# Fused attention and gated hidden layer on one core: weights prepared two per operation in the order of their use, and four of the second chunk's heads on split parts

## The chip, the cores and the metric

One core of a Trainium2 chip runs one program. The metric is the device time of an execution in microseconds. TensorE (PE) multiplies, VectorE (DVE), ScalarE (ACT) and GpSimd (POOL) work on tiles of 128 partitions, SyncE (SP) issues most transfers.

## What is computed

```python
def _attn_ref(q, k, v, n_sink, window):       # q, k, v: (4, 8, 768, 64)
    scores = scale * np.matmul(q, k.transpose(0, 1, 3, 2))
    keep = is_sink | in_window                # n_sink 4, window 128
    scores = np.where(keep, scores, -1000000000.0)
    ...
    return np.matmul(a, v).astype(np.float32) # a: softmax of scores
def _moe_ref(x, w_a, w_b, w_out):             # 3072 tokens, 512 -> 1536 -> 512
    a = x @ w_a
    b = x @ w_b
    return (a * b @ w_out).astype(np.float32)
```

The attention's output, with heads side by side, is the x of the hidden layer. Weights arrive as 64-bit floats (pairs of 32-bit words).

## The kernel before

The 24 tiles of 128 queries are cut into eight chunks: (batch, first tile, tiles) = (0, 0, 4), (0, 4, 2), then six of three tiles. Chunk 0's attention runs alone. After that the hidden layer of a chunk (`moe`) runs with the attention of the next one threaded through it: `between` takes steps of the attention's generator between the products of the hidden units j = 0 to 11.

Precision comes in two ways. The exact way (`parts_exact`) multiplies in 32-bit float. The split way (`parts_split`) rounds an operand to a shorter format (F32R), keeps the rest as a second operand of that format, and adds two products. The hidden layer always uses split operands: three products for each 128 x 128 block of weights (high x high, high x low, low x high). Attention of chunks 0 and 1 is exact, of the others split. In the split way GpSimd makes the high and low parts of k, q and v (`prep_kq`, `prep_v`, tiles ks, qh, ql, vv, vs), and after the transposes of the probabilities ACT makes their high part (tile pt) and DVE their low part.

A weight is a tile of 128 x 512 for each of a, b and o and each hidden unit: 36 in all. `weight_bits` makes a 32-bit float's words out of the 64-bit one's (a shift L297 and a mask L299 on DVE, a conversion L298 on ACT), `weight_sum` adds (L307, DVE), `weight_high` rounds (L313, ACT), and `weight_low` subtracts (L318, DVE). `weights_to` issues one weight's stages at a time, each stage a step behind the one before it, in the order a 0, b 0, o 0, a 1, b 1, o 1 and so on. It is called in the last part of chunk 0's attention (every third step from step 18) and in chunk 0's hidden layer (three times for each hidden unit, through `weights_ahead`). The product of a and b of unit j is used by o's products one unit later, so that o j is wanted after b j+1. All engines work through their queues in order; the order is written by the program and a scheduler that moves independent work ahead.

The PSUM tile t is one bank: in the exact way its first half takes transposes, and its second half (chunk 1) value and sink products. In chunk 1 the value products (L601) and sink products (L623) therefore also appear under the name t.

Of the kernel before, what the change touches and what calls it, by code (L numbers as in the profile page):

```python
# [33 lines left out]
STEP0, STEPS = 18, 3  # L34
AHEAD, LOADS = 3, 9
D0, D1, D2 = 1, 2, 3
WARM = 8
H_MIN = 1.375 * 2.0 ** -12
# [172 lines left out]
UNITS = ((0, 4, "BA"), (1, 2, "AB"), (3, 5, "AB"))  # L211
GROUPS = ((0, 0, 2, 0), (1, 2, 2, 1), (2, 5, 0, 2), (-1, 4, 1, 0))
# [5 lines left out]
class Fast:  # L218
# [14 lines left out]
    def consts(self):  # L233
        nc, cp = self.nc, self.cp
        self.m0 = cp.tile([P, P], F32, name="m0")
        self.m1 = cp.tile([P, SW], F32, name="m1")
        self.mg = cp.tile([P, SW], F32, name="mg")
        self.rel = rel = self.at.tile([P, SW], F32, tag="p", name="rel")
        self.col = col = self.at.tile([P, SW], F32, tag="p", name="col")
        it = dict(allow_small_or_imprecise_dtypes=True)  # L240
        s, b = slice(P, P + NS), slice(P + NS, SW)
        nc.gpsimd.iota(rel[:, b], pattern=[[-1, P]], base=0, channel_multiplier=1, **it)
        nc.gpsimd.iota(rel[:, :P], pattern=[[-1, P]], base=P, channel_multiplier=1, **it)
        nc.gpsimd.iota(rel[:, s], pattern=[[1, NS]], base=0, channel_multiplier=0, **it)
# [7 lines left out]
        self.wt, self.raw, self.wf, self.unchecked = {}, {}, {}, []  # L252
# [34 lines left out]
    def load_weight(self, kind, j):  # L287
        raw = self.wp.tile([P, 2 * DM], I32, tag=f"w_{kind}{j}", name=f"raw_{kind}{j}")
        self.nc.sync.dma_start(raw, self.src(kind)[j].bitcast(I32))
        self.raw[kind, j] = raw  # L290

    def weight_bits(self, kind, j):
        nc, pin = self.nc, self.tc.keep_in_program_order
        rv = self.raw[kind, j].rearrange("p (n c) -> p n c", c=2)
        lo, hi = rv[:, :, 0], rv[:, :, 1]
        f = self.io([P, DM], I32, f"wf_{kind}{j}")
# [4 lines left out]
        self.wf[kind, j] = f  # L301

    def weight_sum(self, kind, j):

        f = self.wf[kind, j]
        lo = self.raw.pop((kind, j)).rearrange("p (n c) -> p n c", c=2)[:, :, 0]
        self.tc.keep_in_program_order(self.nc.vector.tensor_tensor(f, f, lo, op=ALU.add))  # L307
        self.wf[kind, j] = f.bitcast(F32)

    def weight_high(self, kind, j):  # L310
        w = self.wp.tile([P, 2, DM], F32R, tag=f"w_{kind}{j}", name=f"w_{kind}{j}")
        self.wt[kind, j] = (w[:, 0, :], w[:, 1, :])
        self.tc.keep_in_program_order(self.nc.scalar.copy(w[:, 0, :], self.wf[kind, j]))  # L313

    def weight_low(self, kind, j):
        wh, wl = self.wt[kind, j]
        self.tc.keep_in_program_order(
            self.nc.vector.tensor_tensor(wl, self.wf.pop((kind, j)), wh.bitcast(F32), op=ALU.subtract))  # L318
# [71 lines left out]
    def attention(self, b, t0, nt, xf, exact=False, alone=False):  # L390
        parts = self.parts_exact(b, t0, nt, xf, alone) if exact else self.parts_split(b, t0, nt, xf)
        late = [i for i in range(nt) if t0 + i >= 2]
        units = [(h, i) for h in range(H) for i in range(nt)]
        return self.pipeline(units, nt, late, *parts, 3 if alone else 2, 2 if exact else 4, 2 if alone else 1)

    def parts_split(self, b, t0, nt, xf):
# [4 lines left out]
        units = [(h, i) for h in range(H) for i in range(nt)]  # L401
        tps, preps, state, sc, vss, avs, skt = [], {}, {}, {}, {}, {}, {}

        def do_prep(h):
            if h < H:
# [30 lines left out]
        def transposes(h, i):  # L436
            p = state.pop((h, i))
            t = t0 + i
            u = f"{tag}_{h}_{i}"
            n = units.index((h, i))  # L440
            if not tps:
                tps.append(self.ps.tile([P, 4, P], F32, tag="t", name=f"t{u}"))
            tp = tps[0][:, 2 * (n % 2):2 * (n % 2) + 2, :]
            c1, c2, order = UNITS[i]
            parts = {"A": p[:, :P], "B": p[:, P + NS:]}
            if t == 0:
                parts["B"] = p[:, :P]
                order = "B"
            for k, o in enumerate(order):
                nc.tensor.transpose(tp[:, k, :], parts[o], self.ident)  # L450
            n = len(order)
            hs, ls = (self.pt_split()[:, part, c1:c1 + (n - 1) * (c2 - c1) + 1:c2 - c1, :] for part in range(2))
            nc.scalar.copy(hs, tp[:, :n, :])  # L453
            nc.vector.tensor_tensor(ls, tp[:, :n, :], hs.bitcast(F32), op=ALU.subtract)  # L454

        def av(h):
            vv = preps[h][3]
            ps = self.ps.tile([P, 4 * P], F32, tag="av", name=f"av{tag}_{h}")
            pt = self.pt_split()
            products = []  # L460
            for k, sl, ns, c in GROUPS:
# [11 lines left out]
            nc.vector.tensor_tensor(x[mn, 2 * P:], ps[mn, 3 * P:], x[mn, 2 * P:], op=ALU.add)  # L473
# [14 lines left out]
        def sinks_av(g, pr):  # L488
            n = len(late) * P
            ps = self.ps.tile([P, 3 * P], F32, tag="av", name=f"sk{tag}_{g}_{pr}")  # L490
# [6 lines left out]
    def parts_exact(self, b, t0, nt, xf, alone):  # L497
# [7 lines left out]
        units = [(h, i) for h in range(H) for i in range(nt)]  # L505
        preps, state, sc, vss, pts, skt, bank = {}, {}, {}, {}, {}, {}, {}

        def half_bank(second, name):

            if not bank:  # L510
                bank[0] = self.ps.tile([P, 4, P], F32, tag="t", name=name)
            return bank[0][:, 2:] if second else bank[0][:, :2]

        def do_prep(h):
            if h >= H:
                return
# [53 lines left out]
        def transposes(h, i):  # L570
# [16 lines left out]
        def av(h):  # L587
# [3 lines left out]
            else:  # L591
                ps = half_bank(1, f"av{tag}_{h}")
# [12 lines left out]
        def sinks_t(pr):  # L605
# [3 lines left out]
            else:  # L609
                tp = half_bank(0, f"skt{tag}_{pr}")  # L610
# [6 lines left out]
        def sinks_av(pr, _):  # L617
# [3 lines left out]
            else:  # L621
                ps = half_bank(1, f"sk{tag}_{pr}")
# [6 lines left out]
    def pipeline(self, units, nt, late, do_prep, scores, transposes, av, sinks_t, sinks_av, lag, group, early):  # L629

        for h in range(early):
# [39 lines left out]
    def moe(self, row, nt, xf, between, weights_ahead, last, weights_split):  # L671
# [6 lines left out]
        def half(kind, j):  # L678
            wh, wl = self.wt[kind, j]
# [9 lines left out]
        def project(j, gh, gl):  # L689
            wh, wl = self.wt["o", j]  # L690
# [41 lines left out]
    def run(self, scalars, verdict):  # L732
        chunks = CHUNKS
        order = [(k, j) for j in range(NJ) for k in "abo"]
        done, loaded = [0], [0]

        def weights_to(n, ahead):
            while loaded[0] < min(n + ahead, len(order)):
                self.load_weight(*order[loaded[0]])
                loaded[0] += 1  # L740
            while done[0] < min(n + D2, len(order) + D2):
# [8 lines left out]
        pairs = [self.wp.tile([P, 2, nt * P], F32, tag=f"w_{k}{NJ - 1}", name=f"xf0_{k}") for k in "bo"]  # L750
        xf = [x[:, i, :] for x in pairs for i in range(2)]
# [5 lines left out]
        for k, _ in enumerate(first, 1):  # L757
            if k >= STEP0 and (k - STEP0) % STEPS == 0:
                weights_to(done[0] + 1 - D2, 4 + D2)
        for c, (b, t0, nt) in enumerate(chunks):  # L760
            gen = None
            if c + 1 < len(chunks):
                nb, nt0, nnt = chunks[c + 1]
                nxf = self.new_xf(c + 1)
                gen = self.attention(nb, nt0, nnt, nxf, exact=c == 0)
                steps = H * nnt + (6 if c else 5)
            taken = [0]

            def between(s):
                if gen is None:  # L770
                    return
                want = min(steps, -(-steps * (s + 1) // (3 * NJ - 3)))
# [94 lines left out]
```

## Time and profile before

| | |
|---|---|
| median of 3 runs | 802.18 us (800.78 to 804.23) |
| the profiled execution | 800.92 us, span 799.0 us |
| TensorE | busy 785.5 us (98%), granted clock 0.999 |
| VectorE | busy 433.3 us (54%) |
| ScalarE | busy 475.8 us (60%) |
| GpSimd | busy 307.1 us (38%) |

Busy times are from start to end of each instruction; neighbours on one engine overlap a little. Chunk 0's attention fills the first 47 us or so, chunk 0's hidden layer reaches to 179 us, and the other seven chunks take the rest. The whole-program shares of VectorE and ScalarE average a dense first 160 us with a looser remainder.

### The profile page before, as it was taken

To read this page: it belongs to the slowest core of one execution; us is meant where nothing else is said; L and a number is where in the kernel's file an instruction comes from. 1 tells how busy PE (TensorE), PEld (TensorE's weight loads), DVE (VectorE), ACT (ScalarE), POOL (GpSimd) and SP (SyncE) were. 2 spreads that over 40 slices of the span, in tenths; PEclk is the share of its full clock that TensorE was granted. 3 is DMA by queue.
4 is the path that set the end of the run, shared out by engine and by line. 5 is a ranking of instruction groups with operands and counts; after the bars stand their busy time and mean duration, and the time that the engine had idled before them with its cause. 6 is when DMAs were issued, how large, how long until landed. Compare 5 with 4: busy or idle time off the path is not lost.

```text
span 799.0 us, 13573 instructions
## 1 busy us (share of the span) xinstructions
PE 785.5 (98%) x4457; PEld 697.2 (87%) x4457; DVE 433.3 (54%) x1485; ACT 475.8 (60%) x1384; POOL 307.1 (38%) x425
## 2 busy tenths in 40 slices
PE   8989999999999999999999999999999999999997
PEld 5657777779899999999999999999999999999996
DVE  6889988835654565445653555535654457430101
ACT  5877676527764676467764777646764677641111
POOL 1111100416672644546642565606635366201120
PEclk9999999999999999999999999999999999999999
DMA  8868610122221242313333143322333132000001
GB/s 314 298 228 319 205 30 1 41 82 77 61 73 38 79 128 90 104 55 117 102 102 116 42 123 109 91 77 64 114 119 102 54 107 61 1 14 28 1 1 42
DMA packets 44779, 76.12 MB, mean 95 GB/s; under 512 B 4640, under 2 KB 24224, under 8 KB 44704
## 3 DMA queue, kind: packets, MB, share of 16 engines
q1 hardware_dynamic: 41648, 69.70, 27.2%
q10 hardware_dynamic: 3024, 5.51, 1.8%
q8 instruction: 36, 0.59, 0.3%
q14 instruction: 39, 0.32, 0.1%
q0 software_dynamic: 32, 0.00, 0.0%
HBM read 68.90 MB, written 6.29 MB: 94 GB/s over the span
## 4 chain that ended last, share of the span: by engine, by line
PE 92%; DVE 4%; ACT 3%; DMA 1%; issue 1%; POOL 0%; DVEq 0%; POOLq 0%; ACTq 0%
PE a L685 25%; PE o L694 24%; PE b L685 24%; PE t L450 4%; PE s L418 4%; PE av L466 3%; PE s L547 2%; PE av L601 2%; PE t L584 1%; PE t L601 1%; PE sk L491 1%; ACT p L425 1%; DVE g L710 0%; ACT xf L471 0%; DVE xf L472 0%
## 5 line engine op out<-in xcount | busy, mean ns | idle before, releaser
L685 PE MATMUL a<-xh,w_a 128*128 128x384 f32 (+2 forms) x768 | 218.2, 345 | 1.3 <-ACT xh L666 1.0
L685 PE MATMUL b<-xh,w_b 128*128 128x384 f32 (+2 forms) x768 | 215.8, 343 | 0.0
L694 PE MATMUL o<-w_o,gh 128*128 128x512 f32 x576 | 186.9, 404 | 0.0
L685 PEld LDWEIGHTS a<-xh,w_a 128*128 128x128 f32 x768 | 138.8, 188 | 8.2 <-issue 1.7
L715 POOL TENSOR_TENSOR gl<-g,gh 128x384 fp32r<-128x384 f32 (+1 forms) x70 | 68.2, 974 | 201.1 <-ACT gh L713 198.3
L685 PEld LDWEIGHTS b<-xh,w_b 128*128 128x128 f32 x768 | 138.8, 188 | 4.7 <-issue 1.2
L710 DVE TENSOR_TENSOR g<-b,g 128x384 f32<-128x384 f32 (+2 forms) x96 | 53.4, 557 | 146.2 <-PE b L685 133.3
L685 PE MATMUL b<-xl,w_b 128*128 128x384 f32 (+2 forms) x384 | 129.2, 336 | 0.0
L685 PE MATMUL a<-xl,w_a 128*128 128x384 f32 (+2 forms) x384 | 129.2, 336 | 0.0
L694 PEld LDWEIGHTS o<-w_o,gh 128*128 128x128 f32 x576 | 104.0, 188 | 19.3 <-issue 0.8
L694 PE MATMUL o<-w_o,gl 128*128 128x512 f32 x288 | 113.6, 395 | 0.0
L713 ACT CAST gh<-g 128x384 fp32r<-128x384 f32 (+2 forms) x96 | 49.3, 514 | 78.4 <-DVE g L710 76.5
L704 ACT COPY g<-a 128x384 f32<-128x384 f32 (+2 forms) x96 | 45.2, 471 | 72.9 <-PE a L685 70.3
L429 ACT ACTIVATE p<-p,st 128x128 f32<-128x128 f32 (+1 forms) x144 | 71.4, 496 | 26.4 <-DVE st L428 25.5
L425 ACT ACTIVATE p<-p,st 128x128 f32<-128x128 f32 (+1 forms) x144 | 71.6, 497 | 8.5 <-DVE st L423 8.4
L685 PEld LDWEIGHTS a<-xl,w_a 128*128 128x128 f32 x384 | 72.4, 189 | 2.3
L685 PEld LDWEIGHTS b<-xl,w_b 128*128 128x128 f32 x384 | 72.4, 188 | 1.6
L453 ACT CAST pt<-t 128x128 fp32r<-128x128 f32 (+1 forms) x144 | 50.4, 350 | 39.1 <-PE t L450 37.3
L454 DVE TENSOR_TENSOR pt<-t,pt 128x128 fp32r<-128x128 f32 (+1 forms) x144 | 57.2, 397 | 20.7 <-ACT pt L453 19.2
L694 PEld LDWEIGHTS o<-w_o,gl 128*128 128x128 f32 x288 | 54.1, 188 | 13.1 <-DVE gl L715 0.8
L568 POOL COPY sc<-p 128x8 f32<-128x8 f32 x32 | 15.7, 490 | 128.7 <-ACT p L563 86.6
L423 DVE CUSTOM_DVE_ANT_0 p<-s,mg 128x264 f32<-128x264 f32 x96 | 41.1, 429 | 34.2 <-PE s L418 34.0
(141 smaller groups left out, 1287.3 us busy)
## 6 DMA issues: line engine op xcount, KB each, us to landing
qr<-in_qT_dram SPq DMA_DIRECT2D x48, 192.0 KB, 2.6
raw_a<-in_wa_dram SPq DMA_DIRECT2D x12, 512.0 KB, 6.5
raw_b<-in_wb_dram SPq DMA_DIRECT2D x12, 512.0 KB, 6.6
raw_o<-in_wo_dram SPq DMA_DIRECT2D x12, 512.0 KB, 6.6
chk_a<-in_wa_dram SPq DMA_DIRECT2D x24, 256.0 KB, 2.7
chk_b<-in_wb_dram SPq DMA_DIRECT2D x24, 256.0 KB, 2.7
chk_o<-in_wo_dram SPq DMA_DIRECT2D x24, 256.0 KB, 2.8
out_dram<-os ACTq DMA_DIRECT2D x21, 256.0 KB, 2.1
```

Source lines behind the costliest of these rows:

```text
L418: nc.tensor.matmul(ps[:, :w], lhsT=q[:, i * P:(i + 1) * P], rhs=ks[:, c0:c0 + w], start=m == 0, stop=m == 1)
L423: nc.vector.tensor_tensor_reduce(out=p[:, :w], in0=ps[:, :w], in1=m, scale=-0.125, scalar=BIG, op0=ALU.add, op1=ALU.min, accum_out=st[:, 0:1])
L425: nc.scalar.activation(p[:, :w], p[:, :w], AF.Exp, bias=st[:, 0:1], scale=-1.0, accum_out=st[:, 1:2])
L429: nc.scalar.mul(p[:, :w], p[:, :w], st[:, 3:4])
L453: nc.scalar.copy(hs, tp[:, :n, :])
L454: nc.vector.tensor_tensor(ls, tp[:, :n, :], hs.bitcast(F32), op=ALU.subtract)
L685: nc.tensor.matmul(ps[:, :n], lhsT=w[:, ksl], rhs=x[:, :n], start=kk == 0 and i == 0, stop=kk == NK - 1 and i == 2)
L694: nc.tensor.matmul(outs[i], lhsT=g[:, sl], rhs=w, start=j == 0 and k == 0, stop=j == NJ - 1 and k == 2)
L704: nc.scalar.copy(g[:, :n], pa[:, :n])
L710: nc.vector.tensor_tensor(g[:, :n], pb[:, :n], g[:, :n], op=ALU.mult)
L713: nc.scalar.copy(gh[:, :n], g[:, :n])
L715: e.tensor_tensor(gl[:, :n], g[:, :n], gh[:, :n].bitcast(F32), op=ALU.subtract)
```

## The change

Weights are sorted by their use (a 0, b 0, a 1, b 1, o 0, a 2, b 2, o 1, ...). Numbers 2 to 27 of that order are prepared two per operation, 1024 elements instead of 512, through one shared temporary tile; the first two and the last eight stay single. A pair shares one tile. Preparation begins at step 24 of chunk 0's attention instead of 18. In chunk 1, heads 0 to 3 stay exact and heads 4 to 7 take the split way, with one bank for transposes (first half) and products (second half); the four exact heads are spread over the first 18 of the hidden layer's calls and the split ones over the rest.

```diff
-STEP0, STEPS = 18, 3
-AHEAD, LOADS = 3, 9
-D0, D1, D2 = 1, 2, 3
+STEP0, STEPS = 24, 3
+AHEAD, LOADS = 1, 11
+DELAY = 3
+SINGLE, PAIRS = 2, 14
+EXACT, MID = 4, 18
...
+UNITS = {3: ((0, 4, "BA"), (1, 2, "AB"), (3, 5, "AB")), 2: ((0, 4, "BA"), (1, 5, "AB"))}
+GROUPS = {
+    3: ((0, 0, 2, 0), (1, 2, 2, 1), (2, 5, 0, 2), (-1, 4, 1, 0)),
+    2: ((0, 0, 2, 0), (1, 5, 1, 1), (-1, 4, 1, 0)),
+}
...
+        if n == 2:
+            if self.temp is None:
+
+                self.temp = self.wp.tile([P, 2 * DM], I32, tag=f"w{3 * NJ // 2 - 2}", name="wf")
+            f = self.temp
...
+    def attention_of_two(self, b, t0, nt, xf):
+
+        bank = {}
+        first = self.attention(b, t0, nt, xf, exact=True, heads=range(EXACT), bank=bank)
+        second = self.attention(b, t0, nt, xf, heads=range(EXACT, H), bank=bank)
+        next(first)
+        yield
+        n = EXACT * nt
+        for k in range(n + (H - EXACT) * nt + 6):
+            next(first, None)
+            if k >= n - 2 and k != n - 1:
+                next(second, None)
+            yield
...
-        order = [(k, j) for j in range(NJ) for k in "abo"]
+
+        order = self.order = sorted(((k, j) for j in range(NJ) for k in "abo"), key=lambda w: 3 * w[1] + (0, 1, 5)["abo".index(w[0])])
...
-                for d, stage in ((D2, self.weight_low), (D1, self.weight_high), (D0, self.weight_sum), (0, self.weight_bits)):
-                    if 0 <= k - d < len(order):
-                        stage(*order[k - d])
                 done[0] += 1
+                singles = lambda d: 0 <= k - d < len(order) and k - d not in wide
+                if singles(3):
+                    self.weight_low(k - 3, 1)
+                if k % 2 == 0 and k - 2 in wide:
+                    self.weight_low(k - 2, 2)
+                if singles(2):
+                    self.weight_high(k - 2, 1)
+                if singles(1):
+                    self.weight_sum(k - 1, 1)
+                if k % 2 == 1 and k - 1 in wide:
+                    self.weight_sum(k - 1, 2)
+                    self.weight_high(k - 1, 2)
+                if singles(0):
+                    self.weight_bits(k, 1)
+                if k % 2 == 0 and k in wide:
+                    self.weight_bits(k, 2)
...
-                weights_to(done[0] + 1 - D2, 4 + D2)
+                weights_to(done[0] + 1 - DELAY, 4 + DELAY)
...
-                gen = self.attention(nb, nt0, nnt, nxf, exact=c == 0)
-                steps = H * nnt + (6 if c else 5)
+                gen = (self.attention if c else self.attention_of_two)(nb, nt0, nnt, nxf)
+                steps = H * nnt + 6
...
-                weights_to(max(s + AHEAD, done[0] + 1 - D2), LOADS)
+                weights_to(max(s + AHEAD, done[0] + 1 - DELAY), LOADS)
```

Three places show how the queues move. In the rows, p, st and s are a unit's probabilities, statistics and scores (chunk's first tile or batch, head, tile), wf and w a weight under preparation and finished. First VectorE in chunk 0's attention at heads 5 and 6, before:

```order
151 L561 TENSOR_SCALAR p_0_5_3_551<-p_0_5_3_551,st_0_5_3_552 128x264
152 L307 ISA wf_b_518<-raw_b_440,wf_b_518 128x1024
153 L297 TENSOR_SCALAR wf_o_576<-raw_o_442 128x512
154 L559 RECIPROCAL st_0_6_0_583<-st_0_6_0_583 128x1
155 L558 TENSOR_SCALAR st_0_6_1_596<-st_0_6_1_596 128x1
156 L299 SCALAR_TENSOR_TENSOR wf_o_576<-raw_o_442,wf_o_576 128x512
157 L561 TENSOR_SCALAR p_0_6_0_582<-p_0_6_0_582,st_0_6_0_583 128x128
```

and now, at the same place in the attention:

```order
141 L606 TENSOR_SCALAR p_0_5_3_529<-p_0_5_3_529,st_0_5_3_530 128x264
142 L321 TENSOR_SCALAR wf_557<-raw_549 128x512
143 L603 TENSOR_SCALAR st_0_6_0_564<-st_0_6_0_564 128x1
144 L599 ISA p_0_6_1_576,st_0_6_1_577<-s_0_6_1_574,m_106 128x264
145 L599 ISA st_0_6_1_577 128x1
146 L323 SCALAR_TENSOR_TENSOR wf_557<-raw_549,wf_557 128x512
147 L604 RECIPROCAL st_0_6_0_564<-st_0_6_0_564 128x1
```

Before, the third weight (o 0) starts here; now it is the first. Second, TensorE in chunk 1 at head 4's value products (s is a score, t the shared bank), before:

```order
364 L694 MATMUL o_3_806<-w_o_1239,gh_5_1412 128x512 x2
365 L694 MATMUL o_3_806<-w_o_1239,gl_5_1413 128x512
366 L547 MATMUL s_4_6_0_1562<-kx_4_6_1438,qx_4_6_1439 128x264
367 L601 MATMUL t_4_0_0_980<-ptx_4_0_0_979,vx_4_4_1210 64x128 x4
368 L685 MATMUL a_7_1591<-xh_0_787,w_a_1391 128x512
```

and now:

```order
384 L465 MATMUL s_4_6_0_1508<-ks_6_4_1411,qh_6_4_1412 128x264
385 L500 MATMUL t_4_0_0_962<-ident,p_4_4_1_1374 128x128 x2
386 L465 MATMUL s_4_6_0_1508<-ks_6_4_1411,ql_6_4_1413 128x264
387 L739 MATMUL o_0_772<-w_1297,gh_6_1364 128x512 x2
388 L739 MATMUL o_0_772<-w_1297,gl_6_1365 128x512
389 L739 MATMUL o_1_773<-w_1297,gh_6_1364 128x512 x2
390 L739 MATMUL o_1_773<-w_1297,gl_6_1365 128x512
391 L516 MATMUL t_4_0_0_962<-pt,vv_4_4_1211 128x256 x2
392 L516 MATMUL t_4_0_0_962<-pt,vv_4_4_1211 128x128 x4
```

The score is two products on split q, and the head's values six products instead of four, in the same half bank. Third, GpSimd in the same chunk, before:

```order
34 L568 COPY sc_4_0_1_931<-p_4_1_1_1033 128x8
35 L568 COPY sc_4_2_0_1085<-p_4_2_0_1078 128x8
36 L568 COPY sc_4_2_1_1151<-p_4_2_1_1144 128x8
37 L568 COPY sc_4_2_0_1085<-p_4_3_0_1216 128x8
38 L568 COPY sc_4_2_1_1151<-p_4_3_1_1263 128x8
```

and now:

```order
36 L613 COPY sc_4_0_1_904<-p_4_1_1_1008 128x8
37 L613 COPY sc_4_2_0_1075<-p_4_2_0_1068 128x8
38 L366 TENSOR_SCALAR ks_4_4_1202<-kr_4_4_1198 64x400
39 L366 TENSOR_SCALAR qh_5_4_1325<-qr_5_4_1322 128x256
40 L369 TENSOR_TENSOR ks_4_4_1202<-kr_4_4_1198,ks_4_4_1202 64x400
41 L613 COPY sc_4_2_1_1131<-p_4_2_1_1124 128x8
42 L366 TENSOR_SCALAR vv_4_4_1211<-vr_4_4_1209 128x3x64
```

Between and behind the small copies of sink probabilities stand the preparations of heads 4 to 7. From chunk 1's hidden layer on, TensorE's rows are the same as before.

## Rows read from the trace of the kernel before

**Rows 1.** Stretches: busy us (instructions) by engine, then granted clock, DMA share, GB/s

```profile
30.00:62.00 32.00, 29.16 (x144) 17.78 (x144) 27.40 (x101) 24.98 (x69) 5.03 (x9) 1.00 0.76 267
...
120.00:147.00 27.00, 27.00 (x128) 20.80 (x127) 23.92 (x58) 18.09 (x43) 1.57 (x4) 1.00 0.01 2
147.00:163.00 16.00, 16.00 (x79) 12.50 (x78) 12.43 (x16) 6.94 (x15) 11.37 (x15) 1.00 0.30 84
...
180.00:799.00 619.00, 610.71 (x3618) 569.10 (x3616) 290.68 (x1057) 361.84 (x1100) 277.42 (x368) 1.00 0.24 74
```

**Rows 2.** Timeline of TensorE, 13 to 62 us: start, duration, what

```profile
13.39 0.39 PE L547 MATMUL s<-kx,qx 128*128 128x128 f32 x2
...
27.38 0.83 PE L547 MATMUL s<-kx,qx 128*128 128x128 f32 x4
...
45.27 0.71 PE L547 MATMUL s<-kx,qx 128*128 128x264 f32 x2
...
61.26 0.51 PE L685 MATMUL a<-xh,w_a 128*128 128x512 f32 x1 [0.22 <-ACT g L704]
```

**Rows 3.** Chain that ended last, 84 to 104 us: start, duration, what

```profile
84.17 2.77 PE b L685 x12
...
89.73 0.45 PE s L547 x2
90.18 1.02 PE t L601 x8
...
96.23 0.22 PE t L584 x2
...
97.14 0.62 PE t L623 x2
```

**Rows 4.** The same chain at 179 us and at 412 to 424 us

```profile
179.12 1.41 PE a L685 x12
...
412.20 0.25 PE s L418 x2
412.44 0.77 PE av L466 x7
...
423.35 0.30 PE sk L491
```

**Rows 5.** Timeline of VectorE at 63 us

```profile
63.05 0.69 DVE L307 CUSTOM_DVE_ANT_0 wf_b<-raw_b,wf_b 128x1024 uint16<-128x1024 uint16 x1
63.65 0.42 DVE L297 TENSOR_SCALAR wf_o<-raw_o 128x512 int32<-128x512 int32 x1
63.99 0.69 DVE L715 TENSOR_TENSOR gl<-g,gh 128x512 fp32r<-128x512 f32 x1
```

**Rows 6.** Groups on VectorE, 120 to 147 us: busy us, mean ns

```profile
L307 DVE CUSTOM_DVE_ANT_0 wf_b<-raw_b,wf_b 128x1024 uint16<-128x1024 uint16 x3 | 2.1, 685 | 0.0
...
L318 DVE TENSOR_TENSOR w_o<-wf_o,w_o 128x512 fp32r<-128x512 f32 x3 | 2.1, 684 | 0.0
...
L297 DVE TENSOR_SCALAR wf_b<-raw_b 128x512 int32<-128x512 int32 x2 | 0.8, 416 | 0.0
```

**Rows 7.** The same groups, 147 to 163 us

```profile
L318 DVE TENSOR_TENSOR w_o<-wf_o,w_o 128x512 fp32r<-128x512 f32 x2 | 2.3, 1150 | 0.0
L307 DVE CUSTOM_DVE_ANT_0 wf_o<-raw_o,wf_o 128x1024 uint16<-128x1024 uint16 x1 | 1.5, 1517 | 0.0
...
L318 DVE TENSOR_TENSOR w_a<-wf_a,w_a 128x512 fp32r<-128x512 f32 x1 | 1.1, 1091 | 0.0
L307 DVE CUSTOM_DVE_ANT_0 wf_b<-raw_b,wf_b 128x1024 uint16<-128x1024 uint16 x1 | 1.0, 987 | 0.0
...
L297 DVE TENSOR_SCALAR wf_b<-raw_b 128x512 int32<-128x512 int32 x1 | 0.7, 749 | 0.0
```

**Rows 8.** Timeline of GpSimd, two of the small copies in chunk 1

```profile
70.67 2.17 POOL L568 COPY sc<-p 128x8 f32<-128x8 f32 x1 [17.68 <-ACT p L563]
...
107.63 0.19 POOL L568 COPY sc<-p 128x8 f32<-128x8 f32 x1 [5.75 <-ACT p L563]
```

More of the change, by code (lines that the diff above doesn't have):

```diff
@@ L300, in weight_bits, with weight_sum, weight_high, weight_low @@
                                            op0=ALU.bitwise_and, op1=ALU.bitwise_or))
[L301 to L316, printed above, removed]
+        self.wf[k] = f
+    def weight_sum(self, k, n):
+        f = self.wf[k]
+        self.tc.keep_in_program_order(self.nc.vector.tensor_tensor(f, f, self.words(k, n)[0], op=ALU.add))
+    def weight_high(self, k, n):
+        if k % 2 == 0:
+            self.wt[k // 2] = self.wp.tile([P, 2, 2, DM], F32R, tag=f"w{k // 2}", name=f"w{k // 2}")
+        self.tc.keep_in_program_order(self.nc.scalar.copy(self.parts(k, n)[0], self.wf[k].bitcast(F32)))
+    def weight_low(self, k, n):
+        wh, wl = self.parts(k, n)
         self.tc.keep_in_program_order(
-            self.nc.vector.tensor_tensor(wl, self.wf.pop((kind, j)), wh.bitcast(F32), op=ALU.subtract))
+            self.nc.vector.tensor_tensor(wl, self.wf.pop(k).bitcast(F32), wh.bitcast(F32), op=ALU.subtract))
     def check_weight(self, kind, j):
@@ L388, in prep_v, with attention, half_bank, parts_split @@
         return vv
-    def attention(self, b, t0, nt, xf, exact=False, alone=False):
-        parts = self.parts_exact(b, t0, nt, xf, alone) if exact else self.parts_split(b, t0, nt, xf)
+    def attention(self, b, t0, nt, xf, exact=False, alone=False, heads=range(H), bank=None):
+        parts = (self.parts_exact if exact else self.parts_split)(b, t0, nt, xf, alone, heads, bank)
         late = [i for i in range(nt) if t0 + i >= 2]
-        units = [(h, i) for h in range(H) for i in range(nt)]
+        units = [(h, i) for h in heads for i in range(nt)]
         return self.pipeline(units, nt, late, *parts, 3 if alone else 2, 2 if exact else 4, 2 if alone else 1)
-    def parts_split(self, b, t0, nt, xf):
+    def attention_of_two(self, b, t0, nt, xf):
[10 more added lines that the diff above has]
+            yield
+    def half_bank(self, bank, second, name):
+        if not bank:
+            bank[0] = self.ps.tile([P, 4, P], F32, tag="t", name=name)
+        return bank[0][:, 2:] if second else bank[0][:, :2]
+    def parts_split(self, b, t0, nt, xf, alone, heads, bank):
         nc = self.nc
@@ L400, in parts_split, with product @@
         late = [i for i in range(nt) if t0 + i >= 2]
-        units = [(h, i) for h in range(H) for i in range(nt)]
+        units = [(h, i) for h in heads for i in range(nt)]
         tps, preps, state, sc, vss, avs, skt = [], {}, {}, {}, {}, {}, {}
+        def product(name):
+            if bank is None:
+                return self.ps.tile([P, 4 * P], F32, tag="av", name=name)
+            return self.half_bank(bank, 1, name).rearrange("p c q -> p (c q)")
         def do_prep(h):
-            if h < H:
+            if h in heads:
                 preps[h] = *self.prep_kq(b, h, t0, nt), self.prep_v(b, h, t0, nt)
@@ L440, in transposes @@
             n = units.index((h, i))
[L441 to L444, printed above, removed]
+            if bank is not None:
+                tp = self.half_bank(bank, 0, f"t{u}")
+            else:
+                if not tps:
+                    tps.append(self.ps.tile([P, 4, P], F32, tag="t", name=f"t{u}"))
+                tp = tps[0][:, 2 * (n % 2):2 * (n % 2) + 2, :]
+            c1, c2, order = UNITS[nt][i]
             parts = {"A": p[:, :P], "B": p[:, P + NS:]}
@@ L457, in av @@
             vv = preps[h][3]
-            ps = self.ps.tile([P, 4 * P], F32, tag="av", name=f"av{tag}_{h}")
+            ps = product(f"av{tag}_{h}")
             pt = self.pt_split()
             products = []
-            for k, sl, ns, c in GROUPS:
+            for k, sl, ns, c in GROUPS[nt]:
                 if t0 + k >= 0:
@@ L504, in parts_exact @@
         late = [i for i in range(nt) if t0 + i >= 2]
[L505 to L512, printed above, removed]
+        units = [(h, i) for h in heads for i in range(nt)]
+        preps, state, sc, vss, pts, skt = {}, {}, {}, {}, {}, {}
         def do_prep(h):
-            if h >= H:
+            if h not in heads:
                 return
@@ L629, in pipeline @@
     def pipeline(self, units, nt, late, do_prep, scores, transposes, av, sinks_t, sinks_av, lag, group, early):
-        for h in range(early):
+        for h, i in units[:early * nt:nt]:
             do_prep(h)
@@ L678, in half @@
         def half(kind, j):
-            wh, wl = self.wt[kind, j]
+            wh, wl = self.weight(kind, j)
             ps = self.ps.tile([P, 4 * P], F32, tag=kind, name=f"{kind}{tag}_{j}")
```

65 lines of the change are left out of this document (41 added, 24 removed).

## The prediction, made before the changed kernel ran

> **What bounds the kernel now.** I read the stretches first [rows 1]. From 120 us to 163 us, TensorE (PE) is busy for the whole of each stretch at a granted clock of 1.00 (its level of 2.4 GHz). There, a change pays only by what it takes off TensorE's own queue, or loses by a new wait in it. The exception is the start: from 30 us to 62 us TensorE shows 29.16 us busy of 32, while VectorE (DVE) shows 27.40 and ScalarE (ACT) 24.98. Busy hides some waiting there. The first score products of heads 2 and 5 of chunk 0 start at 13.39 and 27.38 us, so three heads take 14.0 us, 4.66 each. The last score of head 7 starts at 45.27 us and takes 0.45: heads 5 to 7 take 18.3 us, 6.1 each, 4.3 us longer for the same products [rows 2]. What is different is that DVE and ACT now also prepare weights. From that last score to the second hidden unit's first product (61.26 us, released by an ACT copy) are 16.0 us. The products queued in between, by the pieces of the chain [rows 3], are 11 exact value products at 0.255 (2.8), 24 of hidden unit 0 at 2.77/12 = 0.23 (5.5), three scores of chunk 1 (1.35), one sink product (0.62) and some 11 transposes at 0.11 (1.2): 11.5 us. So the start loses roughly 4 us ahead of the last score and, with that score's own 0.45 taken off, 4 us behind it to DVE and ACT.
>
> **Part 1, heads 4 to 7 of chunk 1 on split parts.** On the chain, an exact score (0.45 us), a head's exact value products (1.02), and a pair's sink product (0.62, with two small transposes at 0.11 each: 0.84) are all TensorE time [rows 3]. The same work on split parts, from later chunks: a score of two products takes 0.25; seven value products (five of 256 columns, two of 128) take 0.77; a 256-column product takes 1.41/12 = 0.1175 [rows 4]. Hence a 128-column one takes (0.77 - 5 x 0.1175)/2 = 0.09, and the new head (two of 256, four of 128) 0.235 + 0.36 = 0.60. The sinks of four heads become one group: 0.22 of transposes and two products, for which the row of 0.30 (384 columns) is an upper bound and 0.1175 a lower one; I take 0.15. Saved:
> - scores: 8 x (0.45 - 0.25) = 1.6 us
> - values: 4 x (1.02 - 0.60) = 1.7 us
> - sinks: 2 x 0.84 - 0.52 = 1.2 us
>
> Together 4.5 us. If the 128-column products cost as much as 256-column ones and the sinks 0.30 each, it is 3.7; with sinks at 0.1175, 4.6. The transposes of probabilities stay. All of it is on a queue that has no idle time there, so it comes off the end unless a wait takes its place.
>
> **Part 2, the start.** Weight work begins at step 24 of chunk 0's attention instead of 18, in order of use. In DVE's order, the weight operations ahead of the subtraction for the last score fall from 12 to 5 (before 4 shifts, 4 masks, 3 sums, 1 low part; now 2, 2, 1, 0). An operation of 512 elements starts 0.60 us after the one before it, and the shift lets the next start after 0.34 [rows 5]. So 4 x 0.34 + 8 x 0.60 = 6.2 us become 2 x 0.34 + 3 x 0.60 = 2.5 us. Up to the low part of x that hidden unit 0 waits for last, 12.6 us of weight work (seven shifts and masks, six sums, four low parts) become 8.3 (two of each singly, the next pair whole, wide ones taken as twice 0.60 less 0.07, or 0.61 for the shift). If the slower pace of heads 5 to 7 (4.3 us) goes down with this work, 2.6 of it goes away; the tail could give 1 to 2 more, since now only two single weights and one pair must be ready. But what is not done here stands in front of DVE in the first hidden units: the pair (o 0, a 2) must be ready some 7 us after x, behind the 24 products of hidden unit 1 and the rest of unit 0's. DVE needs for it, after x's last low part, a shift, a mask, a sum and a low part of 1024 (0.61 + 3 x 1.13 = 4.0) beside g and gl of unit 0 (1.2), one score (0.35): 5.6 us, and it waits in between for ACT. That just fits. So: bounds 0.5 us (the debt is only moved) and 5 us (nearly all of both losses); I take 3.
>
> **Part 3, the pairs.** Starts 0.60 us apart for 512 elements, where duration is 0.68, leave little fixed cost to save: about 0.07 us an operation, 13 pairs x 4 = 3.6 us of DVE time. In the hidden stretch DVE is not what ends the wait, so this is worth nothing by itself; its cover is TensorE's full queue.
>
> **Part 4, what the split heads put on others.** Per unit a low-part subtraction, and per head one addition, of 256 columns: 12 x 0.33 (half of 0.60 and a little) = 4.0 us of DVE, about what part 3 gives back. GpSimd (POOL) prepares k, q and v of four heads: 26 operations for 8 small copies less. For the next chunk's first two heads it took 14 operations and a copy, 11.37 us [rows 1], so some 20 us here. These fall not on a free stretch, but on the densest of the weight work, before hidden unit 10. What that does, the trace shows at 147 to 163 us, against 120 to 147 us with an all but idle GpSimd: the low part of a weight takes 1150 ns instead of 684, and a sum 1517 instead of 685; over w_o, wf_o, w_a, wf_b and the shift (749 for 416) that is 2 x 0.47 + 0.83 + 0.41 + 0.30 + 0.33 = 2.8 us for 11.4 us of GpSimd work [rows 6, 7]. For 20 us it is about 4.9 us, spread over some five hidden units of 9.6 us in which I count 9.0 us of DVE work: 1.5 pairs at 4.0, g and gl 1.2, 1.6 units at about 0.9, the rest 0.3. DVE then lacks about 5 x (9.0 + 1.0 - 9.6) = 2 us, of which the weights' lead of about one step (1 to 2 us) takes a part. Bounds: nothing, and the whole 4.9; I take 1.5 us of waits on TensorE.
>
> **Sum**: -4.5 - 3.0 + 1.5 = -6.0 us on the profiled execution's 800.92 (span 799.0), which is 1.26 below the median of 802.18: about 796 on the median's scale. From the second chunk's hidden layer on (619 us [rows 1]), TensorE's order is the same as before.
>
> **Rivals.**
> - The start gives nothing: DVE and ACT catch up in hidden units 0 to 2, and TensorE waits for weights there as long as it waited before. Then -4.5 - 0.5 + 1.5 = -3.5: 798.7, within half a per cent. For it: the pair above just fits. Against: TensorE then has eight exact units over six hidden units where DVE has some 2 us a unit to spare.
> - GpSimd starves, and this ends slower. While DVE is dense, a copy on GpSimd that takes 0.19 us elsewhere took 2.17 [rows 8], so it waits behind several DVE operations. If each of 26 operations waited so (2 us), they would need 20 + 52 = 72 us where about 50 are there ahead of the last split scores; TensorE would stand in order at those scores for the difference, 22 us less what DVE works off and frees meanwhile, say half: -7.5 + 11 = +3.5 us, 805.7. It costs from a mean extra wait of 1.2 us an operation (50 - 20 over 26), and outweighs the rest from 1.7. Against: at 147 to 163 us, 15 operations took 11.4 us in all beside dense weight work.
> - GpSimd blocks VectorE for all of its time. Then its 20 us over five hidden units add 4 us to each unit's 9.0 of VectorE, against 9.6 of TensorE: 5 x 3.4 = 17 us, less the weights' lead of 2, so -7.5 + 15 = +7.5, about 810. For it: single operations more than doubled (685 to 1517). Against: over the stretch only a quarter of GpSimd's time came back as VectorE's (2.8 of 11.4 us). The Trainium skill, "SBUF — State Buffer", section "Who interferes with whom", states that the two share a port pair under an exclusive lock and that a VectorE operation with two SBUF inputs and a GpSimd read block each other fully; the trace agrees in kind and differs in size, as just said. By the page the sum would be this +7.5, by the rows the +1.5 of part 4.
> - The split heads do nothing: their products are as long as the exact ones because 128-column products are slow. Then part 1 is 1.6 + 1.2 at most: -4.3, 798. The row of 0.77 for seven speaks against it.
>
> **How the numbers follow.** Forecast (faster by 3.9 to 9.5 us): 0.64. Start gives nothing, or slow products: 0.26, most of it within half a per cent. Starving 0.06, full blocking 0.04. Half a per cent (4 us) is about what a measurement here tells from no change. Range: from -4.6 - 5 = -9.6 (792.6) with a little more, to the first rival with the whole 4.9 of part 4, about 0 (802); 792 to 802.5 leaves out 2 in 10.
>
> **What would show it.** Right: hidden unit 1's first product at 57 to 59 us instead of 61.26; the last split scores without idle time of TensorE ahead of them; chunk 1's first hidden product near 173 us instead of 179.12; weight operations of 1024 at 1.13 us apart; the later chunks as long as before. Wrong: waits of TensorE on o, a or b for w's high or low part between 62 and 160 us, score products released by GpSimd's ks or ql, or value products released by the low part of pt.

## The result and the profile after

The changed kernel took 796.14 us (median of 5, 796.03 to 796.38) against 800.8 for the kernel before (median of 5, 800.78 to 804.23): ratio 0.9929, interval 0.9909 to 0.9949. About 796 was forecast. The profiled execution took 796.14 us with a span of 794.4, 4.6 under the span before. The time came out as forecast, but in part by luck: the forecast's sum was 6.0 us, the gain by spans is 4.6, and two terms of the sum were wrong in opposite directions.

Stretches of the changed kernel (columns as in [rows 1]):

```profile
30.00:62.00 32.00, 30.09 (x162) 21.88 (x162) 28.07 (x91) 24.86 (x64) 4.81 (x8) 1.00 0.78 285
62.00:90.00 28.00, 28.00 (x130) 22.54 (x130) 24.76 (x40) 18.30 (x33) 6.30 (x8) 1.00 0.80 294
90.00:120.00 30.00, 29.51 (x143) 22.27 (x141) 27.48 (x43) 17.17 (x34) 15.31 (x18) 1.00 0.04 13
120.00:147.00 27.00, 25.61 (x123) 19.83 (x124) 25.80 (x60) 19.43 (x48) 7.28 (x8) 1.00 0.11 39
147.00:163.00 16.00, 14.56 (x71) 11.27 (x71) 15.84 (x29) 8.80 (x20) 6.28 (x6) 1.00 0.17 47
```

From 120 to 163 us TensorE was busy without a gap before [rows 1], and from 90 to 120 us as well:

```profile
90.00:120.00 30.00, 30.00 (x144) 22.85 (x144) 27.18 (x68) 19.77 (x46) 2.21 (x5) 1.00 0.18 53
```

Now 3.3 us are missing from 90 to 163 us (0.49 + 1.39 + 1.44), VectorE is at 92 to 99% there, and GpSimd works from 90 to 147 us, where it was nearly idle. TensorE's timeline shows heads 5 to 7 of chunk 0 and the first hidden product (start, duration, what, idle before it and for what):

```profile
27.45 0.83 PE L592 MATMUL s<-kx,qx 128*128 128x128 f32 x4
...
40.50 0.61 PE L592 MATMUL s<-kx,qx 128*128 128x264 f32 x2
...
45.20 0.50 PE L730 MATMUL a<-xh,w 128*128 128x512 f32 x1 [0.82 <-ACT w L335]
```

The chain that ended last shows hidden unit 1 and the start of chunk 1's hidden layer:

```profile
56.45 2.79 PE a L730 x12
...
174.56 1.41 PE a L730 x12
```

- Chunk 0's last score starts at 40.50 us, before at 45.27 [rows 2]: 4.8 us earlier. Heads 5 to 7 take 13.5 us (27.45 to 40.50, and the score's 0.45), before 18.3.
- Hidden unit 1's first product starts at 56.45 us, before at 61.26 [rows 2]: 4.8 earlier. Between these two points lie 15.95 us, before 15.99: the tail gave nothing.
- Chunk 1's hidden layer starts at 174.56 us, before at 179.12 [rows 4]: 4.6 earlier. From unit 1 to there it takes 118.1 us, before 117.9: what the split heads save on TensorE is gone again.
- From there to the end are 619.8 us, before 619.9 (799.0 - 179.12).

TensorE's waits from 62 to 180 us (what waited, for what: sum in us, times, longest):

```profile
PE t L542 <- DVE xf L522: 1.4, 1, 1.4
PE s L465 <- DVE st L470: 0.8, 1, 0.8
PE t L500 <- DVE sct L659: 0.4, 1, 0.4
PE t L500 <- DVE xf L522: 0.4, 1, 0.4
PE t L657 <- ACT xf L648: 0.2, 1, 0.2
```

Together 3.2 us, nearly all of it for VectorE: its row maximum (st), its copy of the sink transposes (sct), its additions into x (xf). None is for a weight, none for GpSimd. VectorE's groups from 100 to 130 us show why it is late (elements, count, busy us, mean ns):

```profile
L330 DVE CUSTOM_DVE_ANT_0 wf<-raw,wf 128x2048 uint16<-128x2048 uint16 x4 | 6.0, 1512 | 0.0
L340 DVE TENSOR_TENSOR w<-wf,w 128x1024 fp32r<-128x1024 f32 x4 | 5.5, 1387 | 1.1 <-ACT w L335 1.1
L323 DVE SCALAR_TENSOR_TENSOR wf<-raw,wf 128x1024 int32<-128x1024 int32 x4 | 5.5, 1368 | 0.0
L321 DVE TENSOR_SCALAR wf<-raw 128x1024 int32<-128x1024 int32 x3 | 3.8, 1275 | 0.0
L760 DVE TENSOR_TENSOR gl<-g,gh 128x512 fp32r<-128x512 f32 x3 | 2.9, 961 | 0.0
```

Their durations without the split heads' GpSimd work follow with the first experiment.

### The profile page after: what moved, and what is told of

The parts are those of the page before. It is cut to its first block, busy times and chain, and to the rows that moved or that the text cites. A ratio compares the mean times of both kernels' runs of the same rounds, so it can differ in the third digit from the quotient of the medians.

```text
span 794.4 us, 13532 instructions
## 1 busy us (share of the span) xinstructions
PE 778.4 (98%) x4445; PEld 695.4 (88%) x4445; DVE 439.5 (55%) x1444; ACT 475.0 (60%) x1368; POOL 328.1 (41%) x443
## 4 chain that ended last, share of the span: by engine, by line
PE 85%; DVE 9%; ACT 3%; issue 1%; DMA 0%; POOL 0%; DVEq 0%; ACTq 0%; POOLq 0%
PE o L739 23%; PE b L730 23%; PE a L730 23%; PE t L500 4%; PE s L465 4%; PE av L516 3%; PE s L592 2%; PE av L646 1%; DVE wf L323 1%; DVE wf L330 1%; DVE wf L321 1%; PE t L629 1%; DVE w L340 1%; DVE pt L504 1%; ACT p L472 1%
## 5 line engine op out<-in xcount | busy, mean ns | idle before, releaser
L730 PE MATMUL a<-xh,w 128*128 128x384 f32 (+2 forms) x768 | 216.4, 344 | 0.8 <-ACT w L335 0.8
L730 PE MATMUL b<-xh,w 128*128 128x384 f32 (+2 forms) x768 | 214.3, 342 | 0.0
L739 PE MATMUL o<-w,gh 128*128 128x512 f32 x576 | 186.2, 403 | 0.0
L730 PEld LDWEIGHTS a<-xh,w 128*128 128x128 f32 x768 | 138.6, 188 | 6.2 <-ACT w L335 1.1
L730 PEld LDWEIGHTS b<-xh,w 128*128 128x128 f32 x768 | 138.6, 188 | 4.1 <-issue 0.7
L730 PE MATMUL a<-xl,w 128*128 128x384 f32 (+2 forms) x384 | 129.1, 336 | 0.0
L730 PE MATMUL b<-xl,w 128*128 128x384 f32 (+2 forms) x384 | 129.1, 336 | 0.0
L739 PEld LDWEIGHTS o<-w,gh 128*128 128x128 f32 x576 | 103.8, 188 | 18.7 <-issue 0.5
L739 PE MATMUL o<-w,gl 128*128 128x512 f32 x288 | 113.8, 396 | 0.0
L476 ACT ACTIVATE p<-p,st 128x264 f32<-128x264 f32 x152 | 75.5, 497 | 28.3 <-DVE st L475 27.3
L472 ACT ACTIVATE p<-p,st 128x264 f32<-128x264 f32 x152 | 75.6, 497 | 10.7 <-DVE st L470 10.6
```

Source lines behind the costliest of these rows:

```text
L472: nc.scalar.activation(p[:, :w], p[:, :w], AF.Exp, bias=st[:, 0:1], scale=-1.0, accum_out=st[:, 1:2])
L476: nc.scalar.mul(p[:, :w], p[:, :w], st[:, 3:4])
L730: nc.tensor.matmul(ps[:, :n], lhsT=w[:, ksl], rhs=x[:, :n], start=kk == 0 and i == 0, stop=kk == NK - 1 and i == 2)
L739: nc.tensor.matmul(outs[i], lhsT=g[:, sl], rhs=w, start=j == 0 and k == 0, stop=j == NJ - 1 and k == 2)
```

## The experiments

**Theory A**: the whole gain is the start, and the split heads' saving comes back as waits. A1: because GpSimd's preparation of the split heads stretches VectorE's weight work. A2: because a pair passes through one temporary tile in series and VectorE stands while ACT rounds. **Rival B**: the split heads pay as forecast, and the start gives only what is left.

**All eight heads of chunk 1 exact**, the rest as changed:

```diff
-                gen = (self.attention if c else self.attention_of_two)(nb, nt0, nnt, nxf)
-                steps = H * nnt + 6
+                gen = self.attention(nb, nt0, nnt, nxf, exact=c == 0, bank=None if c else {})
+                steps = H * nnt + (6 if c else 5)
...
```

(The steps are spread evenly again.) 

> The changed kernel, but with all eight heads of chunk 1 exact, and their steps spread evenly as before. Theory A (the start gives 4.8 us, the split heads nothing net, because what they save on TensorE comes back as waits): the start stays short (unit 1's first product near 56.5 us), the stretch from there to chunk 1's hidden layer stays at 118 us or becomes 118 to 119 without waits of TensorE, and the time is 795.5 to 797. Theory B (the split heads bring their 4.5 us and the pairs cost the waits): 799 to 801, with TensorE waiting on weights in the middle still.

Measured: 796.22 us (795.95 to 796.42), the same as with split heads. Chunk 1's hidden layer starts at 174.65 us, 118.2 behind unit 1. TensorE has no wait from 62 to 163 us. Two stretches:

```profile
90.00:120.00 30.00, 30.00 (x141) 22.91 (x141) 25.17 (x47) 20.77 (x39) 3.49 (x6) 1.00 0.12 33
120.00:147.00 27.00, 27.00 (x132) 20.77 (x131) 23.32 (x49) 16.22 (x35) 3.16 (x5) 1.00 0.11 39
```

Four groups of VectorE, 100 to 130 us:

```profile
L323 DVE SCALAR_TENSOR_TENSOR wf<-raw,wf 128x1024 int32<-128x1024 int32 x5 | 6.1, 1221 | 0.0
L340 DVE TENSOR_TENSOR w<-wf,w 128x1024 fp32r<-128x1024 f32 x4 | 4.9, 1226 | 3.2 <-ACT w L335 3.2
L330 DVE CUSTOM_DVE_ANT_0 wf<-raw,wf 128x2048 uint16<-128x2048 uint16 x4 | 4.9, 1219 | 0.0
L321 DVE TENSOR_SCALAR wf<-raw 128x1024 int32<-128x1024 int32 x5 | 3.4, 688 | 0.0
```

B falls: the split heads are worth nothing in sum. And VectorE's work on four weights stretches by 4 x 0.29 (sum) + 4 x 0.16 (low part) + 4 x 0.15 (mask) + 3 x 0.59 (shift) = 4.2 us when GpSimd is busy beside it, 15.5 us in these 30 instead of 2.9.

**The begin back at step 18**, the rest as changed:

```diff
-STEP0, STEPS = 24, 3
+STEP0, STEPS = 18, 3
```

> The changed kernel with weight work from step 18 again. Theory A (weight work in VectorE's and ScalarE's queues is what slowed heads 5 to 7 and the tail): unit 1's first product returns to 59 to 61 us, the middle gains 1 to 2 us from weights that are further ahead, the time is 797.5 to 800. Rival (the order of use and the smaller demand of unit 0 made the start short, not the step): within 0.5 us of 796.1.

Measured: 801.97 us (801.35 to 803.56), ratio 0.9999 (0.9985 to 1.0013). This is above both expectations: without the later begin, nothing of the change is left. Unit 1 starts at 62.63 us, chunk 1's hidden layer at 180.06, 117.4 later.

**The kernel before with the begin at step 24**, the same line the other way and nothing else: 

> The kernel before with one number changed: weight work begins at step 24 of chunk 0's attention. Theory A (the step alone makes the start short): unit 1's first product at 56.5 to 58 us and a time 3 to 5 us under the kernel before. Rival (the late step needs the order of use, because o 0 stands ahead of a 1): the start is as long as before or longer, since a 1 and b 1 are wanted at once; within 1 us of the kernel before.

Measured: 796.11 us (795.97 to 796.34), ratio 0.9927 (0.9906 to 0.9947), the time of the whole change. Timeline of TensorE:

```profile
40.34 0.61 PE L547 MATMUL s<-kx,qx 128*128 128x264 f32 x2
...
55.49 0.50 PE L685 MATMUL a<-xh,w_a 128*128 128x512 f32 x1 [0.21 <-ACT g L704]
```

The last score starts at 40.34 us here as well, with weights prepared singly. One number in one line makes the gain. Unit 1 starts 1.0 us earlier than in the changed kernel, but chunk 1's hidden layer at 174.60 us, no earlier: the 1.0 us is lost again at once. From 55.49 to 58.05 us seven products take 2.6 us (1.6 at 0.23 each), while the chain passes through ACT's work on weights before the operand gh of the next products is ready:

```profile
55.34 0.62 ACT w_b L313
55.96 0.58 ACT raw_a L298
56.54 0.51 ACT gh L713
57.05 0.04 issue
57.09 0.96 PE o L694 x3
```

**GpSimd's preparation taken away.** Heads 5 to 7 use the k, q and v parts of head 4. 18 of GpSimd's 26 operations for the split heads go (six for each of three heads; the expectation says 19), and the transfers of their inputs; TensorE's and VectorE's work stays.

```diff
+                if bank is not None and h > heads[0]:
+                    preps[h] = preps[heads[0]]
+                    return
```

> The changed kernel, where heads 5 to 7 of chunk 1 use the k, q and v parts that GpSimd made for head 4: it leaves out 19 of 26 GpSimd operations (and their transfers), and all work on the other engines stays. Theory A1 (VectorE's operations of 100 to 158 us are stretched by GpSimd's preparations): weight operations of 1024 come back to about 1.13 us apart, TensorE's idle time of 90 to 163 us (3.3 us) falls below 1.5, and the time is 792.5 to 794. Theory A2 (VectorE is late through its own amount of work and the one temporary tile): 795.5 to 796.5.

Measured: 793.58 us (793.45 to 793.69), 2.6 below the changed kernel. Chunk 1's hidden layer starts at 172.08 us, 115.7 behind unit 1. VectorE's 1024-element operations are back to 1214 to 1222 ns, the shift to 688. Waits of TensorE from 62 to 180 us:

```profile
PE t L545 <- DVE xf L525: 1.4, 1, 1.4
PE t L503 <- DVE xf L525: 0.2, 1, 0.2
```

So A1 holds for about 2.6 us. A wait of 1.4 us remains: the sink product (L542 in the changed kernel) goes into the same half bank as head 7's value products, and waits until VectorE has added those to x. VectorE's timeline of the changed kernel at this place:

```profile
154.84 0.41 DVE L321 TENSOR_SCALAR wf<-raw 128x512 int32<-128x512 int32 x1
155.29 0.41 DVE L535 TENSOR_TENSOR sct<-skt,sct 32x256 fp32r<-32x256 f32 x1
155.73 1.05 DVE L323 SCALAR_TENSOR_TENSOR wf<-raw,wf 128x512 int32<-128x512 int32 x1
156.70 1.53 DVE L340 TENSOR_TENSOR w<-wf,w 128x512 fp32r<-128x512 f32 x1
158.27 0.43 DVE L522 TENSOR_TENSOR xf<-t,xf 64x256 f32<-64x256 f32 x1
```

The value products ended at 154.86 us; the addition comes 3.4 us later, behind four other operations. With heads 5 to 7 unprepared the same two operations stand stretched in front of it, beside GpSimd's preparation of the next chunk's heads, which that run leaves in:

```profile
153.16 1.05 DVE L323 SCALAR_TENSOR_TENSOR wf<-raw,wf 128x512 int32<-128x512 int32 x1
153.75 1.37 POOL L369 TENSOR_TENSOR ks<-kr,ks 64x400 fp32r<-64x400 f32 x1
154.13 1.54 DVE L340 TENSOR_TENSOR w<-wf,w 128x512 fp32r<-128x512 f32 x1
```

Mask and low part take 0.68 us each where GpSimd is idle (150.13 and 151.06 us), so they are 1.2 us too long together. The run therefore does not show that this wait is free of contention: the shared half bank makes the wait possible, and the stretch is nearly as long as the wait. No run took either of the two away.

**Two temporary tiles**, the shift and mask of a pair ahead of the low part of the one before it:

```diff
+            i = k // 2 % 2 if k >= 6 else 0
...
+                swap = k % 2 == 0 and k in wide and k >= 8
+                if swap:
+                    self.weight_bits(k, 2)
```

> The changed kernel with two temporary tiles for the pairs in turn, and the next pair's shift and mask ahead of the low part of the one before, so that ScalarE's rounding of 1.06 us no longer stands between VectorE's sum and low part. Theory A2: 2 us or more come back, 793 to 794.5. Theory A1: VectorE wins up to 1 us in each of some eight pairs but is still stretched: 794.5 to 796.

Measured: 796.1 us (795.94 to 796.27), unchanged. VectorE no longer stands for ACT's rounding (1.1 us in the rows above, now none). The stretch only moves: from 100 to 130 us its low parts grow from 1387 to 1676 ns and its masks from 1368 to 1548, while sums fall from 1512 to 1215 and shifts from 1275 to 835. TensorE's waits from 62 to 180 us are 3.2 us as before. Chunk 1's hidden layer starts 0.9 us earlier, and the rest of the program takes that back but for 0.3 in the span. A2 is not the cause.

**Chunk 0's last small copies on ACT** instead of GpSimd, since one of them stood on the chain at 46.87 us for 2.0:

```diff
-                nc.gpsimd.tensor_copy(sc[h // 2, i][:, h % 2, :], p[:, P:P + NS])
+                (nc.scalar.copy if alone and h > 5 else nc.gpsimd.tensor_copy)(sc[h // 2, i][:, h % 2, :], p[:, P:P + NS])
```

> The changed kernel, with the four small copies of sink probabilities of chunk 0's heads 6 and 7 on ScalarE instead of GpSimd. In the changed kernel's chain one of them takes 2.00 us at 46.87 us and the last sink transposes wait for it. Theory A1 (GpSimd waits behind VectorE's dense weight work): unit 1's first product 1 to 2 us earlier than 56.45, and the time 794 to 795.3. Rival (the copy is long done by the time that VectorE's part of the chain ends): 796 to 796.4.

Measured: 795.72 us (795.49 to 796.36); unit 1 starts only 0.2 us earlier, and the time lies between the two expectations. The copy was hardly what the wait ended with: the value products in front of the sink transposes wait for an ACT copy until 48.16 us here (48.20 in the changed kernel), and the transposes start at 48.74 where they started at 48.92.

**The split heads' roundings on ACT** (12 operations of GpSimd fewer, nothing left out):

```diff
-    def round(self, o, i):
+    def round(self, o, i, act=False):
+        if act:
+            self.nc.scalar.copy(o, i)
+            return
```

> The changed kernel, with the roundings of k, q and v of heads 4 to 7 on ScalarE: 12 of 26 GpSimd operations go, 12 ScalarE operations come. Theory A1: about a third of what leaving out 19 operations gave (2.6 us), so 795 to 795.6, less if ScalarE becomes late. Theory A2: 796 or slower.

Measured: 794.9 us (794.5 to 795.38), 1.2 below the changed kernel. From unit 1 to chunk 1's hidden layer 116.4 us instead of 118.1; the 1024-element sum takes 1273 ns, the shift 773, but the mask 1434 and the low part 1366. A1 again, about half of it and a little more than expected.

**The roundings and the small copies on ACT, with two temporary tiles:** 

> The changed kernel with the two temporary tiles, the four small copies on ScalarE, and the roundings of heads 4 to 7 on ScalarE. If the three add up as theory A1 has it: 793.5 to 794.7. If the waits only move to the last sinks ahead of chunk 1's hidden layer: 795 to 796.

Measured: 794.68 us (794.5 to 795.11). This is the edge of what three gains added up would give, and no clear gain over the roundings alone. These two are the fastest kernels here that compute everything.

**Split heads without pairs**: every weight singly, in the new order.

```diff
-SINGLE, PAIRS = 2, 14
+SINGLE, PAIRS = 2, 1
```

> The kernel after with every weight prepared singly, in the same order (so the split heads without the pairs). If the pairs are worth nothing by themselves even under GpSimd's work (part 3 as predicted), 796.1 plus or minus 0.5. If VectorE's time is what the split heads run short of, the 3.6 us that the pairs save on VectorE (some 0.07 us on each of 52 operations, half of them in 90 to 163 us) come back as waits of TensorE: 797.5 to 800.

Measured: 800.5 us (798.89 to 802.49): 4.4 us above the changed kernel and above both expectations. But single weights are also finished two calls later here than in the kernel before, so the same was run with that kernel's lead (`AHEAD, LOADS = 3, 9`): 

> The kernel after with every weight prepared singly, as in the run of 800.5, but begun two calls earlier in the hidden layer (AHEAD 3, LOADS 9, the lead of the kernel before). If that run lost its 4.4 us because VectorE is short of the time that pairs save, the lead only moves the lack and it stays: 798.5 to 801. If it lost them because single weights under the changed constants are finished two calls later than before, 795.5 to 797.

Measured: 798.69 us (798.16 to 800.0): at the lower end of the first expectation. 2.6 us of the 4.4 stay, and they are VectorE's time: from unit 1 to chunk 1's hidden layer it takes 121.2 us (177.19 - 56.01) instead of 118.1. The lead is worth 1.0 us, all of it in the start: unit 1 starts at 56.01 us with the longer lead and at 57.05 without, and the stretch behind it is as long (121.1). The other 0.8 us between the two medians lies within the scatter: three of the seven times without the longer lead (801.68 to 802.49) have a mean granted clock of 0.994, the others 0.996 to 0.999. TensorE's waits from 62 to 180 us with the longer lead:

```profile
PE t L629 <- DVE xf L670: 2.0, 1, 2.0
PE t L542 <- DVE xf L522: 1.6, 1, 1.6
PE t L500 <- DVE xf L670: 1.4, 1, 1.4
PE s L465 <- DVE st L470: 0.8, 1, 0.8
```

They are 6.1 us with the small one that is not shown, instead of 3.2: with exact heads the pairs are worth nothing (796.22 with, 796.11 without; the order of the weights differs too), beside split heads 2.6 us.

**How far the begin can move.** The kernel before with step 30: 

> The kernel before with weight preparation begun at step 30 of chunk 0's attention instead of 18. If the step only moves VectorE's work and the gain at 24 is what the single late weights allow, TensorE now waits in hidden units 0 to 2 for weights by most of what heads 5 to 7 gain: 796 to 800. If the start still has idle time that a later begin gives back freely, 792 to 794.5.

Measured: 797.6 us (797.28 to 798.96), inside the first expectation. At 30 the later begin costs 1.5 us against step 24. The roundings on ACT with step 30: 

> Roundings of the split heads on ScalarE (as in the earlier run of 794.9) and the begin at step 30. If a later begin is free behind pairs, 791 to 793.5; if the weights are late in hidden units 0 to 2, 795 to 799.

Measured: 802.96 us (800.26 to 804.1), above both expectations. The weights not done at the start are not made up for before the end of the stretch: from 71 us on the chain runs through VectorE nearly without a break, products wait 0.9 and 2.4 us for a weight's low part at 167.56 and 178.20 us, and chunk 1's hidden layer starts at 181.8 us. The profiled execution is the slowest of the ten; the fastest, 800.26 at a mean clock of 0.999, is above both expectations too. The chain, 71 to 78 us:

```profile
71.95 1.15 DVE w L340
73.13 0.69 DVE wf L321
73.88 1.20 DVE wf L323
75.15 1.20 DVE wf L330
76.37 1.06 ACT w L335
77.45 0.58 DVE w L340
```

## Why the prediction was right in its time and wrong in two steps

- **The time, right in part by luck.** The sum was -6.0 us; the spans differ by 4.6 and the profiled executions by 4.8. The start gave 1.8 us more than its term, the split heads' saving came out 0.4 to 1.2 too large, and their waits 1.8 to 2.6 too small, so the sum was about 1.3 too large. The forecast of 796 still met 796.14, because it was put on the median of three scattered times, 1.26 above the profiled one, and the changed kernel hardly scatters. That the scatter would go was not in the prediction.
- **Part 2, the start: right in its mechanism, too small.** -3.0 was taken, -4.8 measured (56.45 against 61.26 us), just inside its bound of 5; the kernel before with step 24 gains 5.8 by unit 1 and keeps 4.8 of it in its span. The step that failed is "if the slower pace of heads 5 to 7 (4.3 us) goes down with this work, 2.6 of it goes away": the loss did not go down in proportion to VectorE's weight work (6.2 to 2.5 us by the prediction's count), it vanished. The three heads take 13.5 us where heads 2 to 4 took 14.0. "The tail could give 1 to 2 more" was wrong: it gave nothing. The first hidden product now waits 0.82 us for ACT to round its weight. The debt that the first rival feared, weights late in hidden units 0 to 2, did not appear in the changed kernel. In the kernel before with step 24 the start of unit 1, with ACT's weight work in front of it, takes back 1.0 us. At step 30 behind pairs products do wait for weights, but at 167.56 and 178.20 us, near the end of the stretch.
- **Part 1, the split heads' TensorE time: right in its mechanism, somewhat too large.** The changed kernel has 3.3 us of TensorE's time free in a stretch of the same length as with exact heads; with the preparation of three heads gone the stretch is 2.5 us shorter and still has 1.6 of waits, 4.1 together. 4.5 was the term, 3.7 to 4.6 its bounds.
- **Part 4, what the split heads put on others: the step that failed most.** 1.5 us of waits were taken, some 3.3 to 4.1 came: between the taken value and the bound of 4.9. GpSimd's added work was as counted: from 62 to 163 us it grew by 18.9 us (35.2 against 16.3 with exact heads), "some 20 us here" by the prediction. The stretch for each microsecond of it was priced somewhat low: 2.8 for 11.4 us, where from 100 to 130 us 4.2 came for 12.6. What failed most is the cover, "of which the weights' lead of about one step (1 to 2 us) takes a part". The weights did keep up: from 62 us on no product waited for one. But VectorE's queue is in program order, so the lateness fell on what stands behind the weights: row maxima, copies and additions that free TensorE's banks. Of the waits, 2.6 us are GpSimd's contention (they go with the preparation of three heads). Some 1.4 fall on the single half bank for products at the last sinks, which the prediction did not have; up to 1.2 of these can be contention as well, with the next chunk's preparation, and this was not separated.
- **Part 3, the pairs: right as put, wrong about the cover.** "Worth nothing by itself" holds with exact heads. But "TensorE's full queue" is no cover once the split heads are there; then pairs are worth 2.6 us. The forecast priced the parts one by one; pairs and split heads are worth together what neither is alone.
- **The rivals.** "The start gives nothing" is refuted by the kernel before with one number changed. "GpSimd starves" did not come about here; with the begin at step 18, two score products waited for its qh and ql, 0.8 and 0.5 us. "GpSimd blocks VectorE for all of its time" would have cost 17 us. The Trainium skill, "SBUF — State Buffer", section "Who interferes with whom", has a VectorE operation with two SBUF inputs and a GpSimd read fully block each other; here 12.6 us more of GpSimd work from 100 to 130 us stretched VectorE's weight work by 4.2, a third and not the whole; [rows 1, 6, 7] had given a quarter. This speaks against pricing GpSimd's whole time, and not against the page: GpSimd's time holds waiting of its own there (the low part of v, 128x192, took 988 ns from 62 to 153 us and 598 ns from 420 us on). "The split heads do nothing" is true of the time and false in its mechanism: their products are shorter, and TensorE waits instead.
- **What was to be seen.** Unit 1 came at 56.45 us where 57 to 59 was said. Behind an operation of 1024 elements the next starts 1.14 us after it where GpSimd is quiet (109.56 to 110.70 us), 1.13 was said. TensorE stands 0.8 us ahead of one of the split scores, and chunk 1's hidden layer starts at 174.56 us where 173 was said: these two pointed at part 4.

Open: how much of the start's gain is VectorE's queue and how much ACT's, which also has weight work to do there, was not separated.

## What to carry to other kernels

Where background work shares an in-order engine with a critical stage, when that work begins can matter more than how it is cut: one constant made the whole gain here, and the same constant moved too far cost part of it again (1.5 us with single weights), or all of it (behind pairs and split heads). A saving on the bounding engine that adds work to two helpers is priced with everything that stands behind that work in their queues, and not with the covered work's own deadline. Run each part of a change alone, and the pair of parts that use the same engine together: the pairs were worth nothing alone and 2.6 us beside the split heads.

## What the runs showed of the hardware

- TensorE's granted clock fell to 0.50, its level of 1.2 GHz, in the profiled executions of the two kernels with the begin at step 30. In the kernel before with step 30 (stretches of 2 us):

```profile
48.00:50.00 2.00, 1.82 (x6) 0.96 (x6) 2.00 (x7) 1.99 (x5) 0.00 (x0) 1.00 0.68 277
50.00:52.00 2.00, 1.47 (x4) 1.23 (x5) 2.00 (x7) 1.81 (x5) 0.00 (x0) 0.71 0.52 157
52.00:54.00 2.00, 2.00 (x6) 1.52 (x6) 2.00 (x7) 1.63 (x3) 0.00 (x0) 0.50 0.86 171
54.00:56.00 2.00, 2.00 (x10) 1.63 (x9) 2.00 (x7) 0.36 (x1) 0.55 (x1) 0.94 0.94 338
```

  Two products of 512 columns take 1.05 us there where they take 0.63 later. Ahead of the fall TensorE stood 0.67 us for ACT's copy of x and 0.66 us for VectorE's row maximum, and the slower products followed. The fall does not come each time: this execution, 798.96 us, is the slowest of four, and the other three (797.28 to 797.78) have a mean clock of 0.999 to 1.000. In the kernel before, the stretch of 58 to 60 us has only 1.05 us busy and the clock stays at 1.00.
- The shift, with one input, suffers most from a busy GpSimd: 1275 ns against 688. The operations with two inputs go from 1219 to 1226 ns to 1368 to 1512.
- The kernel before scatters from 800.5 to 804.8 us over all runs; with nothing but the begin at step 24 it stays within 0.4, and so does the changed kernel. The two with single weights beside split heads scatter again (1.8 and 3.6 us). The scatter goes with the granted clock: every time of the kernel before under 801.4 us in the experiments' rounds has a mean clock of 0.998 to 1.000, and every one over 802.3 one of 0.992 to 0.997. No trace of one of these longer executions was kept, so where the clock fell in them is not shown; nor is why the later begin ends it.
